# Attention's output read back in two transfers a unit instead of eight, with positions set in order by the copies behind the transposes

## The chip, the cores and the metric

The kernel runs on one core of a Trainium2 chip. The metric is the device time of one execution in microseconds (us); lower is better. TensorE is called PE below, VectorE DVE, ScalarE ACT, GpSimd POOL, and SyncE, whose queue issues every DMA of this kernel, SP.

## The reference, cut to what matters

One layer of a model on a sequence of 2048 positions and 512 channels, everything in float32:

```python
xn  = layernorm(x)                                    # x: [2048, 512]
q, k, v = split(xn @ wqkv)                            # 32 heads of 16 channels
idx = pos[:, None] - 2 * arange(8)[None, :]           # each position sees 8 earlier ones, 2 apart
att = softmax(where(idx >= 0, q . k[idx] / 4, -1e9))
s   = (sum_w att * v[idx]) @ wo                       # attention, then the product with wo
h   = relu(xn @ w1 + b1) ** 2                         # 1792 features
g   = silu(h @ w2 + b2)
out = x + s * g
```

## The kernel before

**Matrix products.** Every product is made of float32r operands split in a high part and a low part (`hi` is a copy by ACT, `lo` is source minus `hi`, by POOL or DVE), with three matmuls (`PASSES`) for each pair of operands. A matmul of 128x512 takes PE 0.227 us from start to start, and twice that at half clock.

**Stages.** (1) Norm, transposes and the products with `wqkv`; q, k and v go out to DRAM scratch (`sq`, `sk`, `sv`). (2) `attention()` runs on DVE in eight units of 256 positions each, 16 neighbouring positions by 8 groups of 64 channels laid over the 128 partitions; it starts while stage 1 still runs and lasts until late in stage 4. A unit's result goes to DRAM scratch `so` (`store`), laid out group by group: `so[g, position, 64 channels]`. (3) The product with `w1` (`ups`), in two halves; one half of its result `u` stays on chip, the other goes to DRAM scratch `su` and comes back as tiles `ut`. (4) For each of four chunks `c` of 512 positions, 14 feature blocks `f`: `make_h` squares `u` into `h` (hi and lo), `down(c, f, j)` multiplies by `w2` into four PSUM tiles `pb`; beside it the attention's output is read back (`load_o`, tile `oq`), transposed on DVE (`trans_o`: 32x32 blocks, tile `oTf`), split by ACT and POOL or DVE into `oT`, multiplied with `wo` (`out_product`, tile `pw`), and finished (`finish`: times the gate `z`, plus `x`, out).

**What the change touches.** `load_o(u)` fills `oq` of one unit. Its pool gives `oq` one buffer, so the load of a unit starts when the transposes of the unit before have read theirs. `trans_o(t)` handles half a unit (128 positions: the even or the odd ones, index `e`), `lowo(t)` makes the low part of `oT`. `wo` itself is read by `load_wo` in stage 4, two tiles `rwo` of two transfers each, whose access pattern has a short outer dimension:

```python
    def load_wo(i):
        rwo[i] = p2.tile([P, 2, D], F32, name=f"rwo{i}", tag="rwo", bufs=2)
        for g in range(2):
            row = wo[64 * i + 32 * g:64 * i + 32 * g + 1, :]
            dma(rwo[i][:, g], bass.AP(tensor=row.tensor, offset=row.offset, ap=[[P * D, 4], [D, 32], [1, D]]))
```

**What sets the order.** The program is traced twice. In the first pass every operation goes into a `Book`; `arrange` plays a simple cost model forward (a price for each operation, 600 ns for a DMA issue, 250 bytes a ns on the wire) and picks, engine by engine, the order of the operations, and for operations given to `E` whether DVE or POOL does them. In the second pass that order is fixed: each engine, and SP's queue too, works strictly in it. So a change of the number or size of transfers moves other operations as well. DMA completions are counted on eight semaphores in rotation; an issue waits until the transfer eight issues earlier has landed.

The profile puts every recorded operation on line 159, where `Book.add` issues it, so its rows are told apart by their tiles' names.

Of the kernel before, what the change touches and what calls it, by code (L numbers as in the profile page):

```python
# [11 lines left out]
F32 = mybir.dt.float32  # L12
FR = mybir.dt.float32r
AF = mybir.ActivationFunctionType
# [3 lines left out]
P = 128  # L18
S = 2048
# [11 lines left out]
UP = 256  # L31
NU = S // UP

GR = 8
CH = D // GR
# [407 lines left out]
def trace(ctx: ExitStack, tc: tile.TileContext, plan, x, wqkv, wo, w1, b1, w2, b2, out):  # L443
# [4 lines left out]
    PE, V, A, G, E = (Recorded(book, n, e) for n, e in zip(  # L448
        "PVAGE", (nc.tensor, nc.vector, nc.scalar, nc.gpsimd, dict(V=nc.vector, G=nc.gpsimd))))
    dma = Recorded(book, "S", nc.sync).dma_start  # L450

    def pool(name, stack=ctx, after=(), **k):
        return Pool(book, stack.enter_context(tc.tile_pool(name=name, bufs=1, **k)), name, after)
# [125 lines left out]
    so = dram.tile([GR, S, CH], F32, name="so")  # L579
# [157 lines left out]
    mv, means, rs, shifts, xn, xb, pTs, seen, odd = ({} for _ in range(9))  # L737
# [291 lines left out]
    for a in range(2, NT, 2):  # L1029
        n, t = {2: 2, 4: 1}.get(a, 0), a + 2  # L1030
# [273 lines left out]
    p2 = pool("p2", ctx, (px, pstg, p2a, tpool))  # L1304
# [13 lines left out]
    oqs, oTs = {}, {}  # L1318

    def load_o(u):  # L1320

        if u in oqs:
            return
        oqs[u] = p2.tile([P, UP // 64, 2, 2, CH], F32, name=f"oq{u}", tag="oq")
        for g in range(GR):
            src = so[g, u * UP:(u + 1) * UP, :].rearrange("(b p e) c -> p b (e c)", p=32, e=2)
            dma(oqs[u][32 * (g // 2):32 * (g // 2) + 32, :, g % 2].rearrange("p b e c -> p b (e c)"), src)

    def trans_o(t):
        src = p2.tile([P, 512], F32, name=f"oTf{t}", tag="rwo", bufs=2)  # L1330
        src = src.rearrange("p (g n) -> p g n", g=4)
        V.transpose(out=src.rearrange("p (g h) (b n) -> p b g h n", h=2, n=32),
                    in_=oqs[t // 2][:, :, :, t % 2].rearrange("p b g (h c) -> p b g h c", c=32))
        oTs[t] = p2.tile([P, 2, 4, P], FR, name=f"oT{t}", tag="oT", bufs=3)
        A.activation(oTs[t][:, 0], src, AF.Copy)
        seen[t] = src

    def lowo(t):
        E.tensor_sub(oTs[t][:, 1], seen.pop(t), oTs[t][:, 0].bitcast(F32))

    def out_product(t, ps, cols=slice(0, D)):
        o = oTs[t]
# [50 lines left out]
    for c in range(NCH):  # L1393
        last = c == NCH - 1
        t0 = c * TPC
        for f in range(NF):
# [7 lines left out]
            if c:  # L1404
                if f < 2:
                    finish(t0 - 4 + f, E)
                if f == 2:
                    load_o(c * 2 - 1)
                    load_r(t0 - 2)
                    load_r(t0 - 1)  # L1410
                elif f == 4:
                    trans_o(t0 - 2)
                    trans_o(t0 - 1)
                elif f == 5:
                    lowo(t0 - 2)
                    lowo(t0 - 1)
                elif f == 6:
                    out_product(t0 - 2, psT(f"pw{t0 - 2}"))
                elif f == 7:
                    finish(t0 - 2, E)  # L1420
                    out_product(t0 - 1, psT(f"pw{t0 - 1}"))
                elif f == 8:
                    finish(t0 - 1, E)
            if f >= 7:
                load_o(c * 2)
            if f in (9, 10) and not last:
                load_r(t0 + f - 9)
            if f == 11:
                for i in range(2):
                    trans_o(t0 + i)  # L1430
            if f == 12:
                for i in range(2):
                    lowo(t0 + i)
                load_o(c * 2 + 1)
# [18 lines left out]
        else:  # L1453
# [15 lines left out]
            for j in range(2, TPC):  # L1469
                n = D // 2 if j == TPC - 1 else D  # L1470
# [28 lines left out]
```

## Time and profile before

| | |
|---|---|
| Time, median of 3 runs | 477.96 us (475.67 to 479.42) |
| Profiled execution | 475.35 us, its span 473.6 us |
| Mean granted TensorE clock over the span | 0.996 |
| Busy: PE, DVE, ACT, POOL | 463.6, 403.9, 291.7, 280.5 us |
| `oq` transfers | 64 of 64 KB, median 3.5 us from issue to landing |
| `rwo` transfers | 4 of 256 KB |

Times inside the execution count from the start of its span, and the profiled execution's own time is 1.75 us longer than the span. Stage 4 starts at 266.65 us with the first matmul into `pb`. A row of a timeline has start, length, engine, operation, what it writes and reads, shapes, count and, in brackets, how long the engine stood idle before it and what ended that.

### The profile page before, as it was taken

What the parts mean: (1) busy time and instruction counts of PE and PEld (TensorE: products, weight loads), DVE (VectorE), ACT (ScalarE), POOL (GpSimd) and SP (SyncE); (2) the same over time, 40 slices, a digit from 0 to 9 for tenths busy, and PEclk for the clock granted to TensorE, in tenths of its full rate; (3) what the DMA queues carried; (4) which work ended last, traced back from release to release, by engine and by line L of the source; (5) the groups of instructions that cost most, each with busy time, mean ns of one, the idle gap of its engine ahead of it and who ended that gap; (6) DMA issues with size and microseconds to landing.
All of it is one profiled execution on the core that took longest, in us unless ns stands there. A gap on an engine that the chain in (4) does not pass through costs nothing.

```text
span 473.6 us, 6218 instructions
## 1 busy us (share of the span) xinstructions
PE 463.6 (98%) x2037; PEld 380.6 (80%) x2037; DVE 403.9 (85%) x341; ACT 291.7 (62%) x567; POOL 280.5 (59%) x297
## 2 busy tenths in 40 slices
PE   8999999999999999999999997999999999999996
PEld 6788888888788888888888785788888888888886
DVE  4987977999999998999999984899999999992213
ACT  5756968866564558468584965795249535844311
POOL 2286324336997699956453567876674566376330
PEclk9999999999999999999999998999999999999999
DMA  8799899999689977641860558748894994443102
GB/s 276 210 219 280 287 220 285 253 230 252 184 226 275 261 239 201 227 105 47 209 155 2 156 144 205 193 124 251 174 255 115 259 238 142 146 144 91 45 19 72
DMA packets 77901, 87.78 MB, mean 185 GB/s; under 512 B 6956, under 2 KB 59436, under 8 KB 77868
## 3 DMA queue, kind: packets, MB, share of 16 engines
q1 hardware_dynamic: 77868, 87.38, 69.4%
q8 instruction: 16, 0.26, 0.2%
q14 instruction: 17, 0.14, 0.1%
HBM read 53.75 MB, written 30.47 MB: 178 GB/s over the span
## 4 chain that ended last, share of the span: by engine, by line
PE 89%; DMA 6%; POOL 1%; ACT 1%; DVE 1%; issue 1%; SPq 0%; POOLq 0%
PE pb L159 25%; PE uX L159 16%; PE pq L159 13%; PE pm L159 12%; PE pw L159 9%; PE uZ L159 8%; DMA w2r<-in_B_w 5%; PE uY L159 4%; DMA oq<-so 2%; PE warm L159 1%; SPq L159 0%; PE pxT L159 0%; POOL h L159 0%; DVE wq L159 0%; POOL w L159 0%
## 5 line engine op out<-in xcount | busy, mean ns | idle before, releaser
L159 PE MATMUL pb<-w,h 128*128 128x512 f32 x592 | 152.1, 394 | 3.6 <-POOL h L159 3.5
L159 PEld LDWEIGHTS pb<-w,h 128*128 128x128 f32 x592 | 111.6, 190 | 29.7 <-POOL h L159 5.8
L159 DVE TENSOR_TENSOR pr<-k,qp 128x2048 f32<-128x2048 f32 x32 | 72.8, 2276 | 7.3 <-ACT qp L159 5.6
L159 DVE TENSOR_REDUCE v<-pv 128x256 f32<-128x2048 f32 x32 | 73.0, 2281 | 0.7
L159 DVE TENSOR_TENSOR pv<-v,Lp 128x2048 f32<-128x2048 f32 x32 | 72.8, 2276 | 0.6
L159 DVE TENSOR_REDUCE L<-pr 128x128 f32<-128x2048 f32 x32 | 72.7, 2273 | 0.5
L159 POOL TENSOR_TENSOR h<-ut,h 128x512 fp32r<-128x512 f32 x26 | 33.3, 1295 | 34.6 <-ACT ut L159 33.3
L159 POOL TENSOR_TENSOR h<-u,h 128x512 fp32r<-128x512 f32 (+1 forms) x32 | 33.0, 1050 | 24.1 <-ACT u L159 16.8
L159 PE MATMUL pw<-wot,oT 128*128 128x512 f32 (+1 forms) x204 | 45.5, 376 | 0.0
L159 PEld LDWEIGHTS pw<-wot,oT 128*128 128x128 f32 x204 | 36.8, 188 | 7.1
L159 DVE TENSOR_TENSOR z<-z,pw 128x512 f32<-128x512 f32 (+1 forms) x17 | 11.0, 650 | 26.2 <-ACT z L159 14.4
L159 ACT ACTIVATE ut<-ut 128x512 f32<-128x512 f32 x42 | 24.8, 624 | 12.1 <-DMA ut<-su 12.0
L159 PE MATMUL pq<-wq,XA 128*128 128x512 f32 x122 | 31.5, 391 | 0.3 <-DVE wq L159 0.3
L159 ACT ACTIVATE u<-uX,b1t 128x512 f32<-128x512 f32 x28 | 19.2, 687 | 18.2 <-PE uX L159 14.6
L159 ACT ACTIVATE h<-ut 128x512 fp32r<-128x512 f32 x28 | 16.4, 625 | 22.3 <-PE pb L159 10.5
L159 POOL TENSOR_TENSOR u<-u,more 128x512 f32<-128x512 f32 x14 | 18.2, 1297 | 17.4 <-ACT more L159 16.7
L159 POOL TENSOR_TENSOR oT<-oTf,oT 128x512 fp32r<-128x512 f32 x16 | 20.7, 1295 | 11.3 <-ACT oT L159 11.3
L159 PEld LDWEIGHTS pq<-wq,XA 128*128 128x128 f32 x122 | 22.7, 188 | 5.4 <-DVE wq L159 0.7
L159 ACT ACTIVATE stg<-pm 128x512 f32<-128x512 f32 x30 | 18.0, 599 | 14.3 <-PE pm L159 12.0
L159 ACT ACTIVATE u<-u 128x512 f32<-128x512 f32 (+1 forms) x54 | 26.4, 528 | 0.2
L159 ACT ACTIVATE stg<-pq 128x512 f32<-128x512 f32 x24 | 14.3, 598 | 13.4 <-PE pq L159 10.8
L159 ACT ACTIVATE h<-u 128x512 fp32r<-128x512 f32 (+1 forms) x36 | 17.4, 528 | 5.9 <-PE pb L159 5.8
(166 smaller groups left out, 990.4 us busy)
## 6 DMA issues: line engine op xcount, KB each, us to landing
k<-sk SPq DMA_DIRECT2D x8, 960.0 KB
v<-sv SPq DMA_DIRECT2D x8, 960.0 KB, 7.1
su<-u SPq DMA_DIRECT2D x28, 256.0 KB, 2.5
ut<-su SPq DMA_DIRECT2D x28, 256.0 KB, 4.5
x<-in_A_x SPq DMA_DIRECT2D x16, 256.0 KB, 4.9
sk<-stg SPq DMA_DIRECT2D x8, 512.0 KB, 3.3
sq<-stg SPq DMA_DIRECT2D x8, 512.0 KB, 5.0
sv<-stg SPq DMA_DIRECT2D x8, 512.0 KB, 6.0
```

The costliest lines, as they stand in the source:

```text
L159: ins = f(*a, **k)
```

## The change

A unit of 256 positions is read back with two transfers in place of eight. Before, each of the eight groups of 64 channels had its own transfer of 64 KB into 32 partitions, in pieces of two neighbouring positions (512 bytes). Now one transfer takes four groups (every second one) into all 128 partitions, eight neighbouring positions (2 KB) a partition, 256 KB in all. A partition thus holds other positions than before, so a transposed column `(b, n)` is position `4n + b` of its half unit; the ACT copy and the low part's subtraction, which were plain copies of 512 elements in a row, now go through an access pattern (`positions`) that writes, and for the subtraction also reads, every fourth element of `oT`.

```diff
-        oqs[u] = p2.tile([P, UP // 64, 2, 2, CH], F32, name=f"oq{u}", tag="oq")
-        for g in range(GR):
-            src = so[g, u * UP:(u + 1) * UP, :].rearrange("(b p e) c -> p b (e c)", p=32, e=2)
-            dma(oqs[u][32 * (g // 2):32 * (g // 2) + 32, :, g % 2].rearrange("p b e c -> p b (e c)"), src)
+        oqs[u] = p2.tile([P, 2, UP // 64, 2, CH], F32, name=f"oq{u}", tag="oq")
+        run = UP // 32 * CH
+        for g in range(2):
+            row = so[g, u * UP:u * UP + 1, :]
+            src = bass.AP(tensor=row.tensor, offset=row.offset, ap=[[2 * S * CH, GR // 2], [run, 32], [1, run]])
+            dma(oqs[u][:, g].rearrange("p b e c -> p (b e c)"), src)
 
     def trans_o(t):
         src = p2.tile([P, 512], F32, name=f"oTf{t}", tag="rwo", bufs=2)
-        src = src.rearrange("p (g n) -> p g n", g=4)
-        V.transpose(out=src.rearrange("p (g h) (b n) -> p b g h n", h=2, n=32),
-                    in_=oqs[t // 2][:, :, :, t % 2].rearrange("p b g (h c) -> p b g h c", c=32))
+        V.transpose(out=src.rearrange("p (g h b n) -> p b g h n", g=2, h=2, n=32),
+                    in_=oqs[t // 2][:, :, :, t % 2].rearrange("p g b (h c) -> p b g h c", c=32))
         oTs[t] = p2.tile([P, 2, 4, P], FR, name=f"oT{t}", tag="oT", bufs=3)
-        A.activation(oTs[t][:, 0], src, AF.Copy)
-        seen[t] = src
+        seen[t] = src.rearrange("p (g b n) -> p g b n", g=4, n=32)
+        A.activation(positions(t, 0), seen[t], AF.Copy)
+
+    def positions(t, a):
+        return oTs[t][:, a].rearrange("p g (n b) -> p g b n", b=4)
 
     def lowo(t):
-        E.tensor_sub(oTs[t][:, 1], seen.pop(t), oTs[t][:, 0].bitcast(F32))
+        E.tensor_sub(positions(t, 1), seen.pop(t), positions(t, 0).bitcast(F32))
```

The planned order changes with it from the first `oq` load on. PE's order stays as it was. Three places are shown; in names such as `h0_6`, the numbers are chunk and feature block, and the last number is only a counter.

ACT's queue, in the first chunk of stage 4, before:

```order
L159 ACTIVATE wot_2750<-rwo0_2816 128x512 x2
L159 ACTIVATE qp5_2_1553<-q5_1520 128x512
L159 ACTIVATE u06_2607<-u06_2607 128x2x256
L159 ACTIVATE wot_2750<-rwo1_2841 128x512
L159 ACTIVATE h0_6_2869<-u03_2454 128x512 x2
L159 ACTIVATE u03_2454<-u03_2454 128x2x256 x2
L159 ACTIVATE w28_2821<-w2r9_2844 128x512
L159 ACTIVATE w210_2866<-w2r10_2864 128x512
L159 ACTIVATE wot_2750<-rwo1_2841 128x512
L159 ACTIVATE h0_8_2915<-u04_2589 128x512 x2
```

and with the change:

```order
L159 ACTIVATE wot_2750<-rwo0_2816 128x512 x2
L159 ACTIVATE wot_2750<-rwo1_2841 128x512 x2
L159 ACTIVATE qp5_2_1553<-q5_1520 128x512
L159 ACTIVATE h0_6_2869<-u03_2454 128x512 x2
L159 ACTIVATE u03_2454<-u03_2454 128x2x256 x2
L159 ACTIVATE u06_2607<-u06_2607 128x2x256
L159 ACTIVATE w28_2821<-w2r9_2844 128x512
L159 ACTIVATE w210_2866<-w2r10_2864 128x512
L159 ACTIVATE h0_8_2915<-u04_2589 128x512 x2
```

Both copies of `rwo1`'s halves now stand ahead of `qp5_2` (attention's q for DVE) and of `h0_6`; before, `qp5_2` came first, one copy stood ahead of `h0_6` and the other behind it.

SP's queue at the same time, before:

```order
L159 DMA w2r8_2819<-in_B_w2 128x512
L159 DMA rwo0_2816<-in_A_wo 128x1x512 x2
L159 DMA oq0_2939<-so_155 32x4x128 x8
L159 DMA rwo1_2841<-in_A_wo 128x1x512 x2
L159 DMA w2r9_2844<-in_B_w2 128x512
L159 DMA w2r10_2864<-in_B_w2 128x512
L159 DMA v4_1539<-sv_154 128x1x1920
L159 DMA w2r11_2885<-in_B_w2 128x512
L159 DMA q6_1565<-sq_152 128x1x1024
```

and with the change:

```order
L159 DMA w2r8_2819<-in_B_w2 128x512
L159 DMA rwo0_2816<-in_A_wo 128x1x512 x2
L159 DMA oq0_2939<-so_155 128x1x512 x2
L159 DMA rwo1_2841<-in_A_wo 128x1x512 x2
L159 DMA v4_1539<-sv_154 128x1x1920
L159 DMA w2r9_2844<-in_B_w2 128x512
L159 DMA w2r10_2864<-in_B_w2 128x512
L159 DMA w2r11_2885<-in_B_w2 128x512
L159 DMA q6_1565<-sq_152 128x1x1024
```

Two issues stand where eight stood, and `v4` (attention's v) now goes ahead of `w2r9` and `w2r10`.

DVE's queue with the change, from the second transpose of the first unit on:

```order
L159 STREAM_TRANSPOSE oTf1_3014<-oq0_2939 128x4x4x32
L159 TENSOR_REDUCE v4_1539<-pv4_0_1571 128x256
L159 TENSOR_REDUCE mx5_1560<-L5_1543 128x64
L159 TENSOR_TENSOR h0_12_2994<-u06_2607,h0_12_2994 128x512
L159 TENSOR_TENSOR pv4_1_1574<-v4_1539,Lp4_1541 128x4x2x256
L159 STREAM_TRANSPOSE oTf2_3201<-oq1_3036 128x4x4x32
L159 STREAM_TRANSPOSE oTf3_3205<-oq1_3036 128x4x4x32
```

Between the last transpose of the first unit and the first of the second stand two long operations and two short ones. Before, four long ones stood there: `pv4_1`, its reduction, `pv4_2` and its reduction.

## Prediction

> **What bounds the kernel now.** I read the page's busy line first, then who waited for whom on PE, then PE by stages.
>
> ```profile
> PE 463.6 (98%) x2037; PEld 380.6 (80%) x2037; DVE 403.9 (85%) x341; ACT 291.7 (62%) x567; POOL 280.5 (59%) x297
> PE pb L159 <- POOL h L159: 3.5, 4, 1.7
> ...
> 284.00:296.00 12.00, 9.00 (x31) 6.63 (x31) 5.04 (x4) 6.12 (x12) 8.57 (x7) 0.86 0.88 204
> ...
> 312.00:470.00 158.00, 157.94 (x709) 131.07 (x707) 123.83 (x91) 80.40 (x147) 85.45 (x70) 1.00 0.56 152
> ```
>
> PE is the bound: 463.6 of 473.6 us. From 312 to 470 us it has no gap worth having (157.94 of 158 us). What this change can reach is the opening of stage 4, where PE waited four times for `h`, 3.5 us in all, and where the granted clock (column after the POOL counts) was 0.86 over 12 us: 0.14 x 12 = 1.7 us more. Together that is about 5 us, 1.1% of the time; nothing else can be won on PE. PE's own timeline names the places:
>
> ```profile
> 283.65 1.01 PE L159 MATMUL pb<-w,h 128*128 128x512 f32 x3
> 286.37 7.36 PE L159 MATMUL pb<-w,h 128*128 128x512 f32 x24 [1.71 <-POOL h L159]
> 295.02 1.20 PE L159 MATMUL pb<-w,h 128*128 128x512 f32 x4 [1.29 <-POOL h L159]
> ...
> 307.43 1.43 PE L159 MATMUL pb<-w,h 128*128 128x512 f32 x5 [0.29 <-POOL h L159]
> ```
>
> The waits are for `h0_6` (at 286.37), `h0_8` (295.02) and `h0_12` (307.43). Why was `h0_6` late? ACT and POOL, in their orders:
>
> ```profile
> 277.01 0.58 ACT L159 ACTIVATE qp<-q 128x512 f32<-128x512 f32 x1
> ...
> 282.73 0.63 ACT L159 ACTIVATE wot<-rwo 128x512 fp32r<-128x512 f32 x1 [4.57 <-DMA rwo<-in_A_wo]
> 283.26 1.14 ACT L159 ACTIVATE h<-u 128x512 fp32r<-128x512 f32 x2
> 284.31 1.13 ACT L159 ACTIVATE u<-u 128x512 f32<-128x512 f32 x2
> 285.05 2.51 POOL L159 TENSOR_TENSOR h<-u,h 128x512 fp32r<-128x512 f32 x2 [4.63 <-issue]
> ```
>
> ACT stood 4.57 us at the copy of the first half of `rwo1`, a transfer that `h0_6` doesn't need, and `h0_6` stands behind it. From that landing (282.73) to PE's resumption (286.37) it took 3.64 us.
>
> **The change in the opening.** With the change both halves of `rwo1` and the copy `qp5_2` stand ahead of `h0_6` on ACT. So the question is when the second half lands. SP's timeline and two short windows tell what these transfers cost:
>
> ```profile
> 266.85 1.25 SPq L159 DMA_DIRECT2D rwo<-in_A_wo  x2
> 268.14 7.94 SPq L159 DMA_DIRECT2D oq<-so  x8
> ...
> 273.06 0.30 SPq L159 DMA_DIRECT2D oq<-so  x1
> ...
> 275.78 0.30 SPq L159 DMA_DIRECT2D oq<-so  x1
> 276.24 1.13 SPq L159 DMA_DIRECT2D rwo<-in_A_wo  x2
> ...
> 269.00:270.00 1.00, 1.00 (x6) 0.77 (x5) 1.00 (x1) 1.00 (x5) 0.20 (x1) 1.00 0.27 97
> 273.20:274.00 0.80, 0.80 (x5) 0.65 (x4) 0.80 (x1) 0.80 (x3) 0.80 (x2) 1.00 0.25 93
> ...
> 280.00:281.00 1.00, 1.00 (x6) 0.81 (x5) 1.00 (x1) 0.00 (x0) 0.42 (x1) 1.00 1.04 299
> SPq L159 <- DMA rwo<-in_A_wo: 4.4, 2, 2.4
> DMA to landing us min/median/max: 1.9/3.5/9.9
> ```
>
> The seventh and eighth `oq` issue waited for the two halves of `rwo0` (4.4 us, two waits), so these landed at 273.06 and 275.78, 2.72 us apart. While only they moved, the DMA share was 0.25 to 0.27 at 93 to 97 GB/s; with everything running it was 1.04 at 299 GB/s. A half of `rwo` thus occupies 4 of the 16 DMA engines, and 256 KB at 95 GB/s is 2.7 us; two halves go one behind the other. The new `oq` transfer has the same form as `rwo`'s: outer dimension 4, then 32 rows of 2 KB, into 128 partitions. So I take it to run at the same 2.7 us, on the same four engines. [...]
>
> Behind `rwo0`, then, stand four transfers in one line: `oq0` twice, `rwo1` twice. The second half of `rwo1` lands at 275.78 + 4 x 2.7 = **286.6**. Low end: the first half of `rwo0` (under way alone at 269.0, by the first window) lost time to the 512-byte pieces of `oq0`; at 2.7 us it lands at 271.7 instead of 273.06, 1.3 us earlier, so 285.3. High end: the first half of `rwo1` began when the last old `oq0` transfer was in, 275.78 + 1.9, and landed at 282.73, 5.0 us, with other transfers in flight. `v4` now goes ahead of them; two of four slowed like this give 286.6 + 4.6 = 291.2. I take **288.0**, the middle, since `v4` overlaps about half of the line.
>
> PE resumes 3.64 us later, plus 0.55 for the copy `qp5_2` (rows of 0.58): 288.0 + 4.2 = 292.2, against 286.37: **+5.8 us**. Given back are the waits for `h0_8` and `h0_12`, 1.29 + 0.29 = 1.6 us, since the transfers behind them (`w2r9` to `w2r13`) now have more time: POOL has only three operations of 1.3 us (`wot`, `w28r`, `w210`) between `h0_6` and `h0_8`, while PE's way there is 24 matmuls, 5.4 us. The half clock I take to come once, as before, at no difference. The opening: 5.8 - 1.6 = **+4.2 us**, between +1.5 and +7.4.
>
> **The change after the opening.** The loads. Two transfers of 2.7 us in one line land 1.9 + 5.4 = 7.3 us after their issue, and `oq` has one buffer: a load starts when DVE has transposed the unit before. Between the transposes of units 0 and 1 DVE now has two long operations (2.28 us each, rows below) and two short ones (`mx` 0.66, `h` 0.69), 5.9 us, so DVE stands 1.4 us there. It also starts late, since `qp5_2` frees it and now waits for `rwo1`:
>
> ```profile
> 275.12 1.64 DVE L159 TENSOR_TENSOR h<-u,h 128x512 fp32r<-128x512 f32 x1 [0.71 <-ACT u L159]
> ...
> 293.81 1.71 DVE L159 TENSOR_TENSOR h<-u,h 128x512 fp32r<-128x512 f32 x1 [6.92 <-POOL wot L159]
> ...
> 298.24 0.66 DVE L159 TENSOR_REDUCE mx<-L 128x64 f32<-128x512 f32 x1
> 299.29 0.69 DVE L159 TENSOR_TENSOR h<-u,h 128x512 fp32r<-128x512 f32 x1 [0.38 <-ACT u L159]
> ...
> 312.00:330.00 18.00, 18.00 (x81) 14.89 (x80) 18.00 (x14) 13.34 (x29) 13.18 (x13) 1.00 0.71 207
> 330.00:350.00 20.00, 20.00 (x90) 16.57 (x89) 19.97 (x14) 8.02 (x15) 11.49 (x9) 1.00 0.92 209
> ...
> 370.00:390.00 20.00, 20.00 (x90) 16.57 (x89) 20.00 (x16) 9.42 (x17) 11.54 (x10) 1.00 0.96 246
> ```
>
> DVE would idle from 276.8 to about 289, 12 us, where it idled 0.9 and 6.9 before: 4.5 us later than before. It can't catch up: third column after the sum, DVE is busy 18.00 of 18, 19.97 and 20.00 of 20. With the 1.4 us it runs some 6 us late against PE's 4, and ACT, which works in order, waits for it at `oT`, `qp` and the softmax's `Lp` ahead of later `h`. I put 0 to 3 us on PE for that and take **1**. SP has 48 issues fewer; SP was at the bound only through the landings above, so that is 0.
>
> The copies. ACT writes and POOL reads and writes every fourth element now; no row of theirs has that, so I bound it by DVE's rows:
>
> ```profile
> L159 POOL TENSOR_TENSOR oT<-oTf,oT 128x512 fp32r<-128x512 f32 x16 | 20.7, 1295 | 11.3 <-ACT oT L159 11.3
> L159 DVE TENSOR_TENSOR pr<-k,qp 128x2048 f32<-128x2048 f32 x32 | 72.8, 2276 | 7.3 <-ACT qp L159 5.6
> ...
> L159 DVE TENSOR_TENSOR pv<-v,Lp 128x2048 f32<-128x2048 f32 x32 | 72.8, 2276 | 0.6
> ...
> L159 DVE TENSOR_SCALAR turn<-x,mv,rs 128x512 f32<-128x512 f32 x4 | 4.1, 1028 | 0.5 <-POOL rs L159 0.4
> L159 DVE TENSOR_SCALAR early<-x,mv,rs 128x512 f32<-128x512 f32 x3 | 1.6, 544 | 0.9 <-POOL rs L159 0.9
> ```
>
> `pv` writes every second element and costs what `pr` costs, 2276 ns: no price. `turn`, in runs of 32, costs 1028 against 544 for `early`, 1.89 times. So POOL's low part costs between 1.30 and 2.45 us; below 1.30 is out, since no element less is handled. I take 1.30, because `pv` is the row with single strided elements, and ACT likewise at no price. [...]
>
> **The sum.** +4.2 + 1 = +5.2 us on the profiled execution's 475.35, 480.6. That execution lies 2.6 us under the median 477.96; on the median the forecast is 477.96 + 5.2 = 483.2, so **483 us**. A measurement of this kernel tells about 1%, 4.8 us, from no change, and the forecast lies just beyond it.
>
> **The rivals.** (a) *The new loads run on all 16 engines*, or the line of four is shorter for another reason. Then `oq0` takes 512 KB at 299 GB/s, 1.8 us, as its small pieces did, and `v4` and `w2r9` gain from the free SP queue. With `rwo0` moved up to 271.7 + 2.7 and `rwo1`'s second half at 274.4 + 1.8 + 5.4 = 281.6, PE resumes at 285.8, 0.6 us earlier; the later waits (1.6) and, if the wait becomes too short to halve the clock, 1.7 us go: -3.9 us, 474 us. This case decides from a landing before about 282 on. For it: the 1.29 us wait cost no clock. Against it: the four-engine rows above. Chance 0.10, for a gain over 1% 0.05. (b) *DVE's lag is what PE pays.* Each `oq` load of 7.3 us that lies close to its transposes adds 1 to 3 us of DVE idling, at three units of eight say 4 us more, and PE, with `h` low parts of DVE (`h2_4`, `h2_12`) and ACT's order between them, follows: +9 us, 487. It decides once DVE lies more than about 3 us behind PE. For it: DVE's full columns; against it: `oT` itself is needed late. Chance 0.17. (c) *Strided copies are slow.* 16 x 1.15 = 18 us more on POOL, busy 59%; where an `oT` low part stands right ahead of an `h` low part, 1.15 us each, at three or four places on the path: +4 us beyond the forecast, 487. Chance 0.06. (d) *No change to speak of*: `rwo1` lands where PE's loss and the waits given back cancel, near 284, +/-1 us, 478. It needs the line of four to pass in 2.1 us each, which no row shows. Chance 0.07.
>
> **How the numbers follow.** The forecast (+1.5 to +10, likeliest +5) has 0.60; of that somewhat under half lies within 1%. Faster by over 1%: 0.05, from (a). Slower: 0.32 of the forecast, 0.17 from (b), 0.05 from (c): 0.54 less 0.02 for mild cases of (b): 0.52. Within 1%: the rest, 0.43. The range: 476.5, which leaves out most of (a), to 489, which takes in the forecast's upper end with 0.9 over for (b).
>
> **What would show it.** Right: PE has one wait before `h0_6` of 6 to 9 us, released by POOL's `h`, and ACT's long wait ahead of it is for `rwo`; an `oq` transfer takes 4.5 us and more to land, with a DMA share near 0.25 where it runs alone; the waits at 295 and 307 are gone. Wrong: a DMA share above 0.5 in such a window, PE resuming before 287, or PE gaps after 320 us that outweigh those before.

## The result and the profile after

The changed kernel takes **495.32 us** (median; 492.99 to 499.06) against 476.89 us for the kernel before, run beside it (475.67 to 479.42): a ratio of 1.039, 95% interval 1.030 to 1.047, or +18.4 us. The profiled execution has a span of 494.5 us against 473.6, 20.9 us apart and not 18.4, because the profiled executions (496.27 and 475.35 us) lie off their medians to either side. The prediction had 483.0 us and a range up to 489.0: the direction was right, the size was not.

The page's busy line of the changed kernel:

```profile
PE 471.3 (95%) x2037; PEld 384.3 (78%) x2037; DVE 408.2 (83%) x345; ACT 300.6 (61%) x569; POOL 281.0 (57%) x293
```

Its waits on PE, DVE and ACT (engine, waiting tile, what it waited for: us in total, times, longest):

```profile
PE pb L159 <- POOL h L159: 8.6, 6, 2.0
PE pb L159 <- ACT h L159: 7.8, 2, 7.3
...
DVE oTf L159 <- DMA oq<-so: 22.2, 5, 7.6
DVE pr L159 <- ACT qp L159: 18.8, 3, 14.0
...
ACT ut L159 <- DMA ut<-su: 28.5, 6, 7.4
```

and two of the same waits in the kernel before:

```profile
DVE oTf L159 <- DMA oq<-so: 3.6, 2, 2.8
...
ACT ut L159 <- DMA ut<-su: 12.0, 4, 5.1
```

PE does the same 2037 matmuls, and is busy 7.7 us longer: they ran slower. Its waits for `h` are 16.4 us in place of 3.5. The two differences, 7.7 and 12.9, make the span's 20.9 us, to 0.3. So all of the loss is PE waiting for `h`, and PE running slower behind such waits. PE's timeline shows where (start, length, engine, operation, tiles, shapes, count, idle time before it and what ended that):

```profile
291.04 1.22 PE L159 MATMUL pb<-w,h 128*128 128x512 f32 x2 [7.26 <-ACT h L159]
293.48 6.77 PE L159 MATMUL pb<-w,h 128*128 128x512 f32 x16 [1.22 <-POOL h L159]
...
317.78 5.60 PE L159 MATMUL pw<-wot,oT 128*128 128x512 f32 x24
...
337.18 4.12 PE L159 MATMUL pb<-w,h 128*128 128x512 f32 x10 [1.71 <-POOL h L159]
...
388.11 0.73 PE L159 MATMUL pb<-w,h 128*128 128x512 f32 x2 [0.57 <-ACT h L159]
390.56 2.80 PE L159 MATMUL pb<-w,h 128*128 128x512 f32 x11 [1.72 <-POOL h L159]
...
414.61 7.82 PE L159 MATMUL pb<-w,h 128*128 128x512 f32 x26 [1.98 <-POOL h L159]
...
445.75 4.38 PE L159 MATMUL pb<-w,h 128*128 128x512 f32 x11 [1.71 <-POOL h L159]
```

The first two waits are the opening that the prediction worked out. Behind it, where PE of the kernel before worked 157.94 of 158 us from 312 on, there are now four places with a wait (`h1_4`, `h2_4`, `h2_10`, `h3_4`). The counts tell the clock: 16 matmuls in 6.77 us is 0.42 us each and 11 in 4.38 is 0.40, but 11 in 2.80 (behind the wait at 390.56) is 0.25. (Lengths and counts of the rows end at the window that was asked for.) The windows confirm it (busy time of PE, PEld, DVE, ACT, POOL; granted clock; DMA share; GB/s):

```profile
286.00:300.00 14.00, 7.74 (x18) 5.60 (x19) 9.53 (x6) 9.79 (x17) 7.84 (x6) 0.51 0.57 162
337.00:341.00 4.00, 3.82 (x10) 3.06 (x11) 4.00 (x4) 2.85 (x6) 3.79 (x4) 0.57 1.01 276
390.00:394.00 4.00, 3.44 (x15) 2.86 (x16) 4.00 (x5) 1.70 (x4) 3.06 (x3) 1.00 0.80 267
414.60:419.00 4.40, 4.39 (x12) 3.46 (x13) 4.37 (x3) 1.05 (x2) 2.45 (x2) 0.62 0.76 221
```

Why was `h` late after the opening? The copies that make `h` stand in ACT's queue behind work for attention's output. DVE's timeline at its waits for `oq`, then ACT's ahead of `h2_4` and `h2_10`:

```profile
402.90 0.71 DVE L159 STREAM_TRANSPOSE oTf<-oq 128x512 f32<-128x512 f32 x1 [4.26 <-DMA oq<-so]
...
473.67 1.30 DVE L159 STREAM_TRANSPOSE oTf<-oq 128x512 f32<-128x512 f32 x2 [7.62 <-DMA oq<-so]
```

```profile
386.91 0.60 ACT L159 ACTIVATE qp<-q 128x512 f32<-128x512 f32 x1 [1.45 <-DVE pr L159]
387.45 1.14 ACT L159 ACTIVATE h<-ut 128x512 fp32r<-128x512 f32 x2
...
405.52 0.63 ACT L159 ACTIVATE ut<-ut 128x512 f32<-128x512 f32 x1 [7.43 <-DMA ut<-su]
406.06 2.07 ACT L159 ACTIVATE oT<-oTf 128x512 fp32r<-128x512 f32 x2
```

Ahead of `h` on ACT stand a copy `qp` that waited for DVE, `oT` copies that need a transpose, and squares of `ut` whose load was late. Two readings remain that one profile can't part: DVE's waits for `oq` (22.2 us) hold up what stands behind them, or the few DMA engines that `oq` fills delay the other loads (ACT's waits for `ut`: 28.5 us, 12.0 before).

The copies did get dearer. ACT's half of `oT` costs 1135 ns (626 before, the last row below), POOL's 1612 (1295 before, a row that the prediction shows):

```profile
L159 POOL TENSOR_TENSOR oT<-oTf,oT 128x512 fp32r<-128x512 f32 x16 | 25.7, 1612 | 12.5 <-ACT oT L159 12.5
...
L159 ACT ACTIVATE oT<-oTf 128x512 fp32r<-128x512 f32 x16 | 17.5, 1135 | 6.6 <-DVE oTf L159 5.5 <-PE pw L159 0.9
```

```profile
L159 ACT ACTIVATE oT<-oTf 128x512 fp32r<-128x512 f32 x16 | 9.9, 626 | 14.8 <-PE pw L159 8.9 <-DVE oTf L159 5.8
```

So three theories went on the chip: **1**, the four-engine transfers; **2**, the planned order; **3**, the copies in strides.

### The profile page after: what moved, and what is told of

Read it like the earlier page. It is cut to its first block, busy times and chain, and to the rows that moved or that the text cites. A ratio compares the mean times of both kernels' runs of the same rounds, so it can differ in the third digit from the quotient of the medians.

```text
span 494.5 us, 6157 instructions
## 1 busy us (share of the span) xinstructions
PE 471.3 (95%) x2037; PEld 384.3 (78%) x2037; DVE 408.2 (83%) x345; ACT 300.6 (61%) x569; POOL 281.0 (57%) x293
## 4 chain that ended last, share of the span: by engine, by line
PE 62%; DMA 10%; DVE 10%; ACT 8%; issue 5%; POOL 3%; SPq 1%; POOLq 0%; ACTq 0%; DVEq 0%
PE uX L159 15%; PE pq L159 12%; PE pm L159 11%; PE uZ L159 8%; PE pb L159 7%; DMA ut<-su 4%; PE uY L159 4%; DMA rwo<-in_A_wo 4%; PE pw L159 3%; DVE L L159 3%; DVE pr L159 2%; ACT h L159 2%; DMA oq<-so 2%; ACT ut L159 1%; SPq L159 1%
## 5 line engine op out<-in xcount | busy, mean ns | idle before, releaser
L159 PE MATMUL pb<-w,h 128*128 128x512 f32 x592 | 160.4, 408 | 16.7 <-POOL h L159 8.6
L159 PEld LDWEIGHTS pb<-w,h 128*128 128x128 f32 x592 | 115.7, 197 | 46.6 <-POOL h L159 11.6
L159 POOL TENSOR_TENSOR h<-ut,h 128x512 fp32r<-128x512 f32 x24 | 31.0, 1305 | 37.9 <-ACT ut L159 27.3
L159 POOL TENSOR_TENSOR h<-u,h 128x256 fp32r<-128x256 f32 (+1 forms) x29 | 29.3, 1027 | 37.9 <-issue 18.1
L159 ACT ACTIVATE ut<-ut 128x512 f32<-128x512 f32 x42 | 24.8, 624 | 33.3 <-DMA ut<-su 28.5
L159 POOL TENSOR_TENSOR oT<-oTf,oT 128x512 fp32r<-128x512 f32 x16 | 25.7, 1612 | 12.5 <-ACT oT L159 12.5
L159 DVE STREAM_TRANSPOSE oTf<-oq 128x512 f32<-128x512 f32 x16 | 11.0, 700 | 26.0 <-DMA oq<-so 22.2
```

What stands on the lines that cost most here:

```text
L159: ins = f(*a, **k)
```

## The experiments

Differences below are against the kernel before as it ran beside each experiment (medians 476.9 to 478.6). All keep the changed kernel's plan unless the text says otherwise.

**The same order, transfers with an outer dimension of 128.**

```diff
-            ... ap=[[2 * S * CH, GR // 2], [run, 32], [1, run]])
+            ... ap=[[CH, P], [1, run]])
```

This pattern steps one row of 64 channels from partition to partition, while each piece takes eight rows. So the pieces overlap, and a transfer of 256 KB reads only 135 rows of the scratch, 34 KB.

> The changed kernel, in the same order on every engine, but each of the two transfers of a unit reads 128 rows of 2 KB one after the other from one group, so its outermost dimension is 128 and not 4; the rows are those of one group only, so the positions of the other groups are left out. Theory 1 (the loss is the four-engine transfers, and the lag of VectorE, ScalarE and SyncE behind them): a unit's pair lands within 3 to 6 us of its issue, the waits of VectorE for oq fall from 26 us to under 8, PE's later waits of 1.7 us at h1_4, h2_4, h2_10 and h3_4 go or shrink to under 0.5 each, and the time is 477 to 481. Theory 2 (the order that the change gives ScalarE and SyncE): 489 to 495, the waits stay. Theory 3 (the copies in strides of 16 bytes, ScalarE +0.5 and GpSimd +0.3 us each): 489 to 494, the waits stay.

Measured: 477.42 us, ratio 0.9998 (0.9986 to 1.0010). **The whole loss is gone**, with nothing moved on any engine and the dear copies in place. Waits of PE, and DVE's and ACT's groups:

```profile
PE pb L159 <- ACT h L159: 4.3, 1, 4.3
PE pb L159 <- POOL h L159: 1.4, 2, 1.2
```

```profile
L159 ACT ACTIVATE ut<-ut 128x512 f32<-128x512 f32 x42 | 24.8, 624 | 7.2 <-DMA ut<-su 5.7 <-POOL h L159 1.5
L159 DVE STREAM_TRANSPOSE oTf<-oq 128x512 f32<-128x512 f32 x16 | 11.1, 700 | 1.3 <-DMA oq<-so 1.3
```

DVE's wait fell from 22.2 us to 1.3, ACT's for `ut` from 28.5 to 5.7, and PE's later waits are gone; `oq` took a median of 7.4 us to land, more than the 3 to 6 expected, and that did no harm. By itself the run leaves a rival, the smaller piece of DRAM that is read; the run that reads all positions, further down, speaks against it.

**Plain copies, four engines.** `positions` returns the transposed order as it is.

```diff
-        seen[t] = src.rearrange("p (g b n) -> p g b n", g=4, n=32)
+        seen[t] = src
 ...
-        return oTs[t][:, a].rearrange("p g (n b) -> p g b n", b=4)
+        return oTs[t][:, a].rearrange("p g n -> p (g n)")
```

> The changed kernel, in the same order, its transfers on four engines, but oT's copies write in the order of the transpose, so output positions are permuted. ScalarE's copy falls back to 0.63 us, GpSimd's subtraction to 1.30. Theory 1: 488 to 494, VectorE still waits over 20 us for oq. Theory 3: 477 to 482. Theory 2: 492 to 495.

Measured: 495.09 us, ratio 1.036 (1.033 to 1.039): no gain over the changed kernel's 495.32. ACT's copy is back at 626 ns, POOL's at 1350, and DVE waits as long as ever:

```profile
L159 DVE STREAM_TRANSPOSE oTf<-oq 128x512 f32<-128x512 f32 x16 | 11.1, 701 | 27.0 <-DMA oq<-so 23.3 <-issue 3.7
```

**Both edits at once** (128-row transfers and plain copies): only the order is left.

> The changed kernel's order with both of the former's edits: transfers whose outermost dimension is 128 (one group's positions alone) and plain copies (permuted positions). What is left of the loss is the order alone. Theory 1: 476 to 480, like the kernel before. Theory 3: 476 to 480 too. Theory 2: 486 to 495.

Measured: 477.42 us, ratio 1.0002 (0.9988 to 1.0016). Theory 3 has fallen, and theory 2 as stated: with quick transfers this order costs nothing.

**The kernel before, its eight transfers put on four engines: a miss.**

```diff
-            src = so[g, u * UP:(u + 1) * UP, :].rearrange("(b p e) c -> p b (e c)", p=32, e=2)
+            row = so[g, u * UP:u * UP + 1, :]
+            src = bass.AP(... ap=[[UP // 4 * CH, 4], [2 * CH, 32], [1, 2 * CH]])
```

> The kernel before, in its own order, but each of the eight transfers of a unit is written with an outermost dimension of 4 (32 rows of 4 KB within it as before's 32, in permuted order), so that it runs on four engines. Theory 1: the units' transfers take 2.7 us per 256 KB in one line as after, rwo's second half lands at 287 to 292 in place of 283, and the time is 484 to 496. Theories 2 and 3: 476 to 481.

Measured: 478.02 us, ratio 1.0004 (0.9988 to 1.0021). It says nothing of theory 1, because the transfers landed as before (64 issues, median 3.4 us to landing, before 3.5). A block is 32 pieces of two rows, 64 rows, and the next block starts 64 rows on, so the two dimensions can be read as one of 128. The repeat leaves two rows of overlap between blocks:

```diff
-            src = bass.AP(... ap=[[UP // 4 * CH, 4], [2 * CH, 32], [1, 2 * CH]])
+            src = bass.AP(... ap=[[(UP // 4 - 2) * CH, 4], [2 * CH, 32], [1, 2 * CH]])
```

> The kernel before in its order, each of a unit's eight transfers (64 KB) from four blocks of rows that overlap a little, so that they don't fold into one dimension; if that puts them on four engines, a unit's eight take about 5.4 us of those engines in one line as after, rwo's second half lands at 289 to 293 and the time is 484 to 496. If they still run on sixteen: 476 to 480, and nothing is learnt of the engines.

Measured: 488.72 us, ratio 1.023 (1.021 to 1.025), +11.1 us in the unchanged order with unchanged copies. The last unit's transfers were issued up to 450.3 us, and the DMA share was 0.30 at 80 GB/s from 452 to 454 us. DVE stood 13.8 us for transfers ahead of its transposes (5.3 of them put down to `oq`), and PE's and ACT's waits look like the changed kernel's:

```profile
PE pb L159 <- POOL h L159: 8.8, 7, 2.6
PE pb L159 <- ACT h L159: 4.7, 2, 4.2
...
ACT ut L159 <- DMA ut<-su: 29.4, 6, 6.2
```

**The opening and the rest apart.** The 128-row transfers for the first unit alone, then for the seven later ones alone (`if u == 0`, `if u > 0` on the access pattern).

> The changed kernel in its order, with the 128-row transfers for the first unit alone (one group's positions); the seven later units keep four engines. Theory 1a (two separate losses: the opening, where rwo's second half stands behind the first unit's oq, 5.9 us, and four later waits of PE, 15 us, each made by the oq of its own unit): the opening goes, the later waits stay, 487 to 491. Theory 1b (the later waits are the opening's lag, carried on by VectorE and ScalarE, which work in order): nearly all of it goes, 477 to 481.

Measured: 492.54 us, ratio 1.031 (1.030 to 1.033), **+14.8 us**. Without the opening's line of transfers the later waits stay as they were:

```profile
PE pb L159 <- POOL h L159: 8.3, 6, 1.7
PE pb L159 <- ACT h L159: 4.9, 3, 4.1
...
DVE oTf L159 <- DMA oq<-so: 20.4, 4, 9.0
```

It came out 1.5 us above the top of theory 1a's expectation and far above 1b's.

> The mirror of the one before: the first unit's pair stays on four engines, the seven later ones are 128-row transfers on sixteen. Theory 1a: the opening's 5.9 us stay, the later waits go, 482 to 485. Theory 1b: the opening's lag is carried on and the later waits stay, 490 to 495.

Measured: 480.80 us, ratio 1.0063 (1.0048 to 1.0078), **+3.1 us**, 1.2 below the expectation. PE's opening is the changed kernel's (it resumes at 290.95 us, there at 291.04), and after it nothing waits:

```profile
290.95 1.22 PE L159 MATMUL pb<-w,h 128*128 128x512 f32 x2 [7.55 <-ACT h L159]
```

The two add up: 14.8 + 3.1 = 17.9 of 18.4 us. So the losses are separate, and the opening isn't carried on.

**An outer dimension of 8.**

```diff
-            ... ap=[[2 * S * CH, GR // 2], [run, 32], [1, run]])
+            ... ap=[[20 * CH, 8], [CH, 16], [1, run]])
```

> The changed kernel in its order, each of a unit's transfers with an outermost dimension of 8 (overlapping rows of one group): 8 engines, by estimate half of the 2.7 us, 1.35 us each. If the loss grows in proportion to the transfers' time beyond that on sixteen (0.7 us), a third of it is left: 482 to 486. If it decides only once VectorE's lag passes the slack that PE has, little is left: 477 to 480.

Measured: 479.74 us, ratio 1.0039 (1.0022 to 1.0056): +2.0 us, a ninth of the loss and not a third. DVE still waits, 9.5 us:

```profile
L159 DVE STREAM_TRANSPOSE oTf<-oq 128x512 f32<-128x512 f32 x16 | 11.0, 699 | 13.1 <-DMA oq<-so 9.5 <-POOL L L159 2.0 <-POOL h L159 1.6
```

So here DVE stood 9.5 us for `oq` at a cost of 2 us, where 22 us came with a loss of 18. That fits a slack that is used up first; two points don't show where it ends.

**Waits taken away, transfers kept.** The plan is made as before; in the program that runs, the transposes read the bias tile.

```diff
-                    in_=oqs[t // 2][:, :, :, t % 2].rearrange("p g b (h c) -> p b g h c", c=32))
+                    in_=(oqs[t // 2][:, :, :, t % 2] if plan is None else b2t.rearrange("p (g b c) -> p g b c", g=2, b=4))
+                    .rearrange("p g b (h c) -> p b g h c", c=32))
```

> The changed kernel in its order, its transfers on four engines issued as before, but VectorE's transposes read the broadcast bias b2 in place of oq, so that no instruction waits for oq and attention's output is left out of the result. If VectorE's waits for oq, which hold up the work queued behind them in order, are what PE pays after the opening (15 of the 18 us): 478 to 483, with the opening's wait for rwo left. If it is the crowding of the four engines, which delays the loads of u and with them ScalarE: 488 to 494, with ScalarE's waits for ut still near 28 us.

Measured: 484.66 us, ratio 1.014 (1.011 to 1.017), +6.1 us: between the two expectations, 1.7 us above the one and 3.3 below the other.

```profile
PE pb L159 <- ACT h L159: 7.7, 1, 7.7
PE pb L159 <- POOL h L159: 3.2, 4, 1.2
...
ACT ut L159 <- DMA ut<-su: 19.4, 6, 5.6
```

PE's first wait is the opening's. So 18.4 - 6.1 = 12.3 us of the loss go when no transpose waits for `oq`. Of the 6.1 left (by the interval 5.4 to 8.0), 3.1 are the opening, by the run with 128-row transfers for the later units, and some 3 are what four busy engines cost without anyone waiting for `oq`; `ut` is late there still (19.4 us on ACT, 5.7 with an outer dimension of 128). So both readings hold a part. How large each is stays open, because the edit also frees SP. In the changed kernel SP's queue, with loads of `ut` in it, stood until transposes had released `oq`:

```profile
SPq L159 <- DVE oTf L159: 8.0, 2, 6.6
```

Here those two waits are gone, and the second unit's pair is issued at 300.72 us and not at 307.28. The 12.3 us are DVE's waits and the earlier issues together.

**The planner told the price.** The transfers of the changed kernel as they are, but the planner counts 2.6 times their bytes, so it reckons them at 96 GB/s where it reckoned 250.

```diff
             dma(oqs[u][:, g].rearrange("p b e c -> p (b e c)"), src)
+            book.ops[-1].moved *= 2.6
```

> The changed kernel as it is, but the planner counts the oq transfers at 2.6 times their bytes (97 GB/s where it reckons 250), so it issues them earlier or puts other work ahead of what waits for them; their time on four engines stays. If the order planned on a wrong price is what turns slow transfers into PE's waits: 478 to 485. If the four engines' line is the bound whatever the order: 490 to 496.

Measured: 480.27 us, ratio 1.0058 (1.0042 to 1.0075), +2.7 us. With four-engine transfers throughout, most of the loss is gone; DVE waits 9.4 us for `oq`:

```profile
PE pb L159 <- ACT h L159: 4.5, 1, 4.5
PE pb L159 <- POOL h L159: 2.0, 4, 1.2
...
DVE oTf L159 <- DMA oq<-so: 9.4, 3, 6.8
```

Theory 2 comes back in another form: the order isn't bad in itself, it is planned for transfers of 250 bytes a ns, and alone on the wire these run at 93. The order changed on DVE, ACT, POOL and SP from the first stage on, so which of its moves counts stays open.

**All positions, an outer dimension of 32.** Four transfers a unit, each filling 32 partitions from two groups; the order is planned anew, and differs mostly on SP.

```diff
-        for g in range(2):
-            row = so[g, u * UP:u * UP + 1, :]
-            src = bass.AP(... ap=[[2 * S * CH, GR // 2], [run, 32], [1, run]])
-            dma(oqs[u][:, g].rearrange("p b e c -> p (b e c)"), src)
+        for k in range(GR // 2):
+            row = so[2 * k, u * UP:u * UP + 1, :]
+            src = bass.AP(... ap=[[run, 32], [S * CH, 2], [1, run]])
+            dma(oqs[u][32 * k:32 * k + 32].rearrange("p g b e c -> p g (b e c)"), src)
```

> The changed kernel with all positions, but four transfers a unit in place of two: each fills one quarter of the partitions from two groups, 32 partitions outermost, pieces of 2 KB, 16 engines. The planned order is another one. If the four engines are the whole loss: 475 to 480; if the planned order counts for several us: anywhere from 480 to 486.

Measured: 479.43 us, ratio 1.0037 (1.0020 to 1.0054). The loss is gone but for 1.7 us, with every position read once; a transfer of 128 KB landed in a median of 3.8 us, and how many engines it used isn't shown. In the opening PE waits 6.5 us for ACT's `h`, behind `rwo`, where it waited 4.3 with the 128-row transfers.

**`rwo` in the same form**, with these `oq` transfers and, by itself, in the kernel before. `rwo` always had the outer dimension of 4. Both are planned anew; in the second the order of ACT, DVE, POOL and SP changes from the start of stage 4 on.

```diff
-        for g in range(2):
-            row = wo[64 * i + 32 * g:64 * i + 32 * g + 1, :]
-            dma(rwo[i][:, g], bass.AP(... ap=[[P * D, 4], [D, 32], [1, D]]))
+        for k in range(4):
+            row = wo[64 * i + P * k:64 * i + P * k + 1, :]
+            dma(rwo[i][32 * k:32 * k + 32], bass.AP(... ap=[[D, 32], [32 * D, 2], [1, D]]))
```

> As the quarters for oq, and rwo too in four transfers a tile of 32 rows outermost, so that no load of this stage is left on four engines. The opening's wait for rwo (before 3.6 us of PE's idle time at h, with one half-clock stretch of 3.4 us) should go: 471 to 476, against 475 to 480 with oq alone. If rwo's landing isn't what the opening waits for once oq is quick, no difference: 475 to 480.

> The kernel before with rwo alone in four transfers of 32 rows outermost. The opening's 3.6 us of waits and 1.7 us of half clock go where the theory of four-engine loads is right: 471 to 475. If the opening is bound by the DMA engines' total, 476 to 479.

Measured: 469.70 us with the change (ratio 0.9832, 0.9818 to 0.9845), **469.38 us** without it (0.9825, 0.9811 to 0.9838). Both beat the kernel before by 8 us, more than expected. In the second, PE's only wait in the opening is 0.2 us and the clock stays full (window of 12 us, after the POOL counts), where the kernel before had 3.5 us and a clock of 0.86:

```profile
PE pb L159 <- POOL h L159: 0.2, 1, 0.2
```

```profile
284.00:296.00 12.00, 12.00 (x55) 9.94 (x54) 10.50 (x10) 8.15 (x16) 10.04 (x9) 1.00 1.03 221
```

The spans differ by 5.8 us (473.6 and 467.8), of which those waits and that clock are 3.3 + 1.7 = 5.0; another 2.4 us of the medians' 8.2 lie between the profiled execution of before and its median. How much of the 8 us is `rwo`'s landing and how much the new order isn't told apart. The two times are alike: with `rwo` read so, four transfers a unit in place of eight bring nothing.

## Why the prediction missed

- **Four engines** (right). Alone on the wire the last `oq` pair of the changed kernel has a DMA share of 0.25 at 93 GB/s, as `rwo` had, and an outer dimension of 128 undoes the loss (477.42 us), with `oq` landing 2.9 us after its issue at the least; how many engines it used isn't shown. With an outer dimension of 8 the share was 0.43 while `oq` was landing. That `oq` and `rwo` would stand in one line on the same four engines was my estimate, and no row of the kernel before shows it; in the changed kernel, with `rwo0`, `oq0` and `rwo1` issued one behind the other, the share was 0.27 at 99 GB/s from 268 to 276 us, no more than for one of them alone. The changed kernel, then the run with 8:

```profile
468.00:473.00 5.00, 5.00 (x24) 4.14 (x23) 0.00 (x0) 2.19 (x4) 2.17 (x2) 1.00 0.25 93
```

```profile
454.00:456.00 2.00, 2.00 (x11) 1.65 (x10) 0.00 (x0) 2.00 (x4) 0.24 (x1) 1.00 0.43 137
```

- **The opening, +4.2** (inside its range, with the clock term wrong). ACT takes the second half of `rwo1` at 289.32 us, after a wait ahead of each half:

```profile
286.93 0.63 ACT L159 ACTIVATE wot<-rwo 128x512 fp32r<-128x512 f32 x1 [10.09 <-DMA rwo<-in_A_wo]
289.32 0.63 ACT L159 ACTIVATE wot<-rwo 128x512 fp32r<-128x512 f32 x1 [1.76 <-DMA rwo<-in_A_wo]
```

  The forecast was 288.0, within 285.3 to 291.2. PE resumed in two steps, at 291.04 for ACT's high part and at 293.48 for POOL's low part (forecast: one step, at 292.2, released by POOL), and the waits at 295 and 307 are gone. But "The half clock I take to come once, as before, at no difference" was wrong: from 286 to 300 us, of which the first 5 are the wait, the clock was 0.51, and 16 matmuls at 0.42 us instead of 0.23 are 3.1 us where the kernel before paid 1.7. At the first `pw` PE was 5.9 us behind (317.78 against 311.87). The run with only the opening left on four engines agrees: its profiled execution, 480.89 us, lies 5.5 above the one of before, 475.35. The medians differ by 3.1 us, since 475.35 is 2.4 below the median of before there. The forecast of 4.2 lies between, and with a clock term that was wrong that is in part luck.
- **The step that failed: "I put 0 to 3 us on PE for that and take 1".** It measured 14.8 us, with 128-row transfers for the first unit. The mechanism stood in the prediction as rival (b), DVE's lag is what PE pays, at a chance of 0.17 and a price of 4 us above the forecast. Two things were under-sized. I sized DVE's wait for `oq` as 1.4 us at one unit, from a pair that lands 7.3 us after its issue with four engines to itself; it was 22.2 us in five waits. The pair that SP issued at 391.78 us (timeline below, the second number is the length of its two issues) released DVE at 402.90, 11.1 us on, with `ut` loads in flight. And PE's price for a wait isn't the wait alone: three of the four later places (337, 414 and 445 us) also cost a stretch of half clock.

```profile
390.53 1.19 SPq L159 DMA_DIRECT2D ut<-su  x2
391.78 1.16 SPq L159 DMA_DIRECT2D oq<-so  x2
```

- **DVE can't catch up** (right, but the lag from the opening alone was harmless). With only the first unit on four engines DVE starts its last `pr` at 386.4 us, 6.4 later than in the kernel before (380.0), near the 6 us of the prediction, and PE waits nowhere after the opening. With the later units on four engines too, in the changed kernel, it starts at 396.4, 10 us later still. The prediction counted a wait at one of these units only, and gave the lag 1 us with no look at which `h` stands behind which of DVE's results in ACT's queue.
- **Strided copies at no price** (wrong row, no harm). `pv` on DVE was the wrong neighbour for ACT, 1135 ns against 626, and for POOL, 1612 ns against 1295, which lies between the bounds of 1.30 and 2.45 us. The upper bound was shaky: `turn`'s 1028 ns is the mean of four operations from 549 to 1400. ACT has a `turn` of its own in the kernel before (below), at 830 ns where its copy `qp` of the same size took 580; that row spoke against no price. POOL's price is a quarter more, in a subtraction that writes every fourth element and reads one of its two inputs so. Rival (c) didn't occur: plain copies gained nothing with the slow transfers (495.09 us), and the dear ones cost nothing with the quick (477.42).

```profile
L159 ACT ACTIVATE turn<-x,shift,rs 128x512 f32<-128x512 f32 x8 | 6.6, 830 | 0.0
```

- **Rival (a)**, 16 engines, gave 474 us; with an outer dimension of 128 on the chip it was 477.4. The step is its landing, 281.6 for `rwo1`'s second half: ACT took it at 286.64, and PE resumed at 288.37, for ACT's `h` behind the same two copies of `rwo`, which had stayed on four engines. With `rwo` in four transfers too, four `oq` transfers a unit and a new order, it was 469.7.

```profile
288.37 1.22 PE L159 MATMUL pb<-w,h 128*128 128x512 f32 x2 [4.33 <-ACT h L159]
```

## What to carry to other kernels

Read the outermost dimension of each transfer's access pattern before its size: with one of 4 a load of 256 KB moved at 93 GB/s and a DMA share of 0.25, four of 16 engines' worth, and it cost 18 us here as a change. Four loads of `wo` had the same form in the kernel before, with PE busy 98% of the span; written otherwise, with the order planned anew, they gave 8 us. Where a planner sets the order, a transfer that it prices wrongly can cost more than its own delay, since other work is queued in the belief that it has landed: with the price corrected 2.7 us were left of 18.4. Correct the price or the transfer. When an engine that is busy 100% of a stage falls behind, follow its results into the in-order queues that feed the bound engine before giving the lag a small number.

## What the runs showed of the hardware

- A wait of PE of 1.7 us may or may not cost clock: 1.71 us ahead of 337.18 and 1.98 ahead of 414.61 were followed by windows at 0.57 and 0.62, 1.72 ahead of 390.56 by a window at 1.00. There PE had worked 0.73 us between two waits. What decides isn't shown.
- At half clock a matmul took 0.42 to 0.43 us from start to start (at 296.21 and 296.63 us in the changed kernel, at 288.13 and 288.56 in the kernel before), 1.9 times the 0.227 at full clock. The half clock came in pieces of about 3.4 us. In the changed kernel the clock was 0.51 over 337.1 to 340.6, 415.6 to 419.1 and 446.3 to 449.8 us, and over four times that length at the opening, 285.9 to 299.7; in the kernel before over 287.0 to 290.5. Behind 340.6 it was 1.00 again. Two of the four executions of the changed kernel had a mean clock of 0.976 (496.3 and 499.1 us), two 0.986 (493.0 and 494.4 us): the half-clock stretches differ from one execution to the next.
- ACT's copy that writes every fourth element of float32r costs 1135 ns, in order 626; POOL's subtraction that writes so and reads one of its two inputs so, 1612 against 1295; DVE's transpose is the same 700 ns in either form.
- Two dimensions that follow one another without a gap behaved as one: an outer 4 by 32 pieces that join landed in 3.4 us and cost nothing, and 4 by 32 with an overlap cost 11.1 us.
